# Another order for the first third of a planned kernel: small rows beside a weight's third

## The chip, the cores and the metric

The kernel runs on one core of a Trainium2 chip. The metric is the device time of one execution in microseconds (us), taken as the median of several runs. A core has five engines with a queue each, and each works its queue in order: PE multiplies matrices (PEld is its weight load), DVE, ACT and POOL do elementwise work, SP only issues transfers. ACT issues transfers too. The transfers themselves are carried by 16 DMA engines.

## What is computed

The first half is a linear attention with decay over 4 x 8 heads, 768 positions and 48 dimensions a head:

```
for t in range(S):
    cur = einsum('bhd,bhe->bhde', u * k[t], v[t])
    y[t] = einsum('bhd,bhde->bhe', r[t], state + cur)
    state = w[..., None] * state + einsum('bhd,bhe->bhde', k[t], v[t])
```

The second half takes y as x of shape (4, 768, 384), normalises each row with a gain g, and adds a two-layer network: `x + relu(norm(x) @ w1) @ w2`, with w1 of 384 x 1536 and w2 of 1536 x 384. Inputs and output are fp32; the kernel multiplies in bf16.

## The kernel before, in words

The positions are cut into 24 chunks of 128, six for each of the four batch entries. All work is written as small named steps. A string, PLAN, lists 895 of them as `name,index,engine`; the kernel emits them in exactly that order, and each engine and each transfer queue keeps it. The last letter gives the engine where there is a choice: v is DVE, s is ACT, g is POOL; for a transfer, s means that ACT issues it and a dash that SP does. So the order is a schedule, made ahead by a search and written out by hand.

The steps of one chunk i, in the order of their data:

- RA and RB load the two halves of r (96 KB each; packed rows, L410), KA and KB those of k for the chunks 0 to 3; LK loads all of k of a later chunk (L406), LV all of v (L437, 192 KB).
- SR and SK multiply r and k by powers of the decay (L217) into a bf16 tile `sc`; CV makes v bf16.
- TR transposes both on PE (L458, L462), TCr and TCk copy the result from PSUM to `trs` (L212). For the chunks 0 to 3, TB transposes k back (L476) and KC copies it into `sc` (L214), since the packed load has its rows in another order.
- Q multiplies the two transposed tiles, AT makes the scores on PE (L489), AM (in halves: AMa, AMb) masks them (L499).
- S on PE adds up the state and the weight of the present position (L520, L527, L533), CC copies the latter, ZU and ZD scale the state.
- VB is v times that weight (L552), Y the output of the attention on PE (L562, L570), X the sum of both (L577).
- SQ sums squares (L584), XN centres the row (L592), LT transposes it on PE (L626), XT copies it.
- UP is one part of the first layer (L641; PSUM tile `hp`), RL its relu (L657 on ACT, L659 on DVE), DN one third of the second layer (L669), OT the final sum (L725), STO the store.

Ahead of the chunks stand the constants. LE loads w (4 rows), LC 1 loads u (4 rows, L254) and LC 2 loads g (3 rows, L252), all tiny. LN takes the logarithm of w (L227), WBR spreads it over all partitions by a matmul (L240), PW, EK and ER make exponents of it, FKP and FR their exponentials (L357, L354). CR copies w into the tile `rows`, CT turns `rows` into columns with a matmul (L264), and CP copies those out. WBK is the other spreading matmul (L246), and FK and FN are its exponentials (L332, L337). WL makes the decay over a chunk (L368, L371). BD, UW and UGC make the rest.

The weights come in three parts of 768 KB each: LW1 n for w1 (L378), LW2 n for w2 (L395). SW scales w1 to bf16 in nine parts (three a third; L385 on ACT, L387 on DVE, L389 on POOL), CW copies w2 to bf16 in six. UP 0 needs the third 0 of w1, UP 2 the third 2, UP 1 the third 1; DN 0, 1 and 2 need the thirds of w2 of these numbers.

DU is a matmul of zeros, 512 columns wide (L316). It computes nothing; it keeps PE at work where nothing else is ready.

Transfers share eight semaphores in turn. A transfer therefore waits, on the engine that issues it, until the transfer eight places earlier in the plan has landed; what is queued behind it on that engine waits too.

The end of the function, which makes the order binding:

```
for step in PLAN.split():
    name, i, e = step.split(",")
    steps[name](int(i), e)
...
for ins in list(nc.cur_bb.bb.instructions)[traced:]:
    for chain in [ins.engine] + ["dma"] * ("dma" in type(ins).__name__.lower()):
        if chain in last:
            tc.add_manual_dep(ins, last[chain].name, in_order, reason="order of the plan")
        last[chain] = ins
```

Of the kernel before, what the change touches and what calls it, by code (L numbers as in the profile page):

```python
# [30 lines left out]
AT,3,- DN,0,- TB,3,- RL,18,s RL,1,s RA,5,- LK,5,- RA,8,s SQ,1,s ZU,2,v VB,2,v Q,3,v RB,5,- UP,17,- DN,1,- X,2,v SQ,2,s
UP,16,- RS,1,g SR,4,g CV,3,s RL,17,s KC,3,v AM,3,v LV,4,- RL,16,s DN,2,- RB,6,s RS,2,g SK,5,g RB,8,s XN,2,v Y,3,- LT,2,-
S,3,- CC,3,s LK,8,- SK,4,v OT,0,v XT,2,v RB,7,- LK,6,- VB,3,v DN,4,- TR,4,- RA,6,- UP,33,- TCr,4,s TCk,4,s ZU,3,v X,3,v
RL,33,s CV,4,s SQ,3,s UP,32,- DN,5,- LV,5,- RB,12,- RA,7,- XN,3,v Q,4,v SR,5,v AT,4,- LV,6,- S,4,- TR,5,- TCr,5,s DN,6,-
AM,4,v ZU,4,v OT,1,v SK,6,v SR,6,v TCk,5,s Y,4,- UP,34,- LT,3,- RB,11,- RB,13,s RL,32,s RA,12,s XT,3,s SR,8,g CC,4,s LK,7,s
VB,4,g AT,5,- DN,8,- RB,9,- Q,5,v TR,6,- DN,9,- S,5,- UP,49,- RL,34,s TCk,6,s AM,5,v SK,8,v UP,48,- LK,9,- TCr,6,s CV,5,s
RA,9,s RL,49,s RL,48,s TR,8,- AT,6,- CC,5,s TCk,8,s LV,7,- RA,13,- SR,7,v X,4,v RA,10,s RS,3,g CV,6,g VB,5,g Q,6,v XN,4,v
Y,5,- TCr,8,s AM,6,v UP,50,- DN,10,- S,6,- LT,4,- X,5,v SK,7,g XN,5,g RB,10,s XT,4,v SQ,4,s LK,10,s LK,14,s CC,6,s AT,8,-
Y,6,- RS,4,g SK,9,g ZU,6,v OT,2,v RL,50,v TR,7,- UP,66,- SQ,5,s VB,6,g RS,5,g CV,7,g DN,12,- TCk,7,s SR,9,g SR,10,g RL,66,s
TCr,7,s UP,65,- UP,64,- LT,5,- AM,8,v RA,16,- Q,8,v Q,7,v LK,11,s AT,7,- X,6,v XT,5,v RL,65,v DN,13,- LV,8,- LV,10,- RA,11,-  # L40
S,7,- DN,14,- CC,7,s AM,7,v OT,3,v ZU,7,v TR,9,- UP,81,- TCk,9,v SK,10,v Y,7,- VB,7,g STO,0,s XN,6,s RL,64,s TCr,9,s DN,16,-
RL,81,s ZD,7,v CV,8,g LV,9,- X,7,v S,8,- UP,80,- DN,17,- AT,9,- TR,10,- Y,8,- SK,11,v RA,14,- DN,18,- UP,82,- CC,8,v Q,9,v
XN,7,s LV,11,- ZU,8,v RL,80,s LK,12,s TCr,10,s CV,9,s TCk,10,s SQ,6,s VB,8,g SR,11,g AM,9,v LT2,6,- LV,13,s STO,1,- ZD,8,g STO,2,-
OT,4,v X,8,v LK,13,- LV,12,s SR,12,g S,9,- AT,10,- STO,3,- AM,10,v ZU,9,v TR,11,- SR,13,g DN,20,- Y,9,- RA,17,- XN,8,s TCr,11,s
RL,82,s CV,10,s CC,9,s TCk,11,v DN,21,- RB,16,s ZD,9,v Q,10,v Q,11,v VB,9,v LK,17,- UP,99,- AT,11,- RL,99,s S,10,- UP,96,- DN,22,-
UP,101,- CC,10,s X,9,v VB,10,g RL,96,s ZU,10,v OT,5,v SK,12,g CV,12,g RL,101,v S,11,- UP,97,- XN,9,s LT2,8,- CC,11,s TR,12,- Y,10,-
UP,100,- AM,11,v CV,11,g ZD,10,g SK,13,g CV,13,g RL,97,s UP,98,- TCr,12,s SQ,7,s TCk,12,v X,10,v RL,100,v XN,10,v Q,12,v RL,98,s DN,24,-
AT,12,- TR,13,- Y,11,- DN,25,- UP,113,- S,12,- RS,6,g LK,15,s RB,14,- LK,16,- LV,14,- RB,15,- RA,15,- VB,11,g LR,18,s RB,17,s RL,113,s
DN,26,- UP,115,- SQ,8,s TCk,13,v TCr,13,v X,11,v AM,12,v SK,14,g Q,13,g SR,14,g XN,11,s RL,115,s UP,114,- CC,12,v OT,6,v ZU,12,v LV,15,s
TKD,14,- SK,15,v SQ,11,s RL,114,s AT,13,- S,13,- DN,28,- TR,14,- UP,112,- DN,29,- TCr,14,s SR,15,g UP,116,- CC,13,v AM,13,v SK,16,v VB,13,g  # L50
RL,112,v ZU,13,v DN,30,- OT,7,v SQ,9,s SQ,10,s VB,12,g UP,117,- Y,13,- DN,32,- AT,14,- LT2,10,- LV,16,- TKD,15,- TKD,16,- ZD,13,g STO,4,s
Q,14,v LK,19,- LR,19,- X,13,v RL,117,v XN,13,v RS,7,g RL,116,s CV,14,s S,14,- DN,33,- TR,15,- Y,12,- SK,17,v TCr,15,s SR,16,g UP,131,-
X,12,v AM,14,v TKD,17,- DN,34,- UP,130,- STO,5,s RL,131,s LV,18,- RL,130,s XN,12,s LR,20,- Q,15,g TR,16,- AT,15,- Y,14,- CC,14,s CV,16,s
OT,8,v LT2,12,- SR,17,v RS,8,g TCr,16,v VB,14,v CV,15,g ZU,14,v LK,18,- UP,128,- DN,36,- UP,129,- DN,37,- Q,16,g S,15,- DN,38,- TR,17,-
AM,15,v X,14,v RL,128,v CC,15,s TCr,17,s SQ,13,s ZD,14,g SQ,12,s VB,15,g RL,129,v Q,17,g Y,15,- AT,16,- UP,132,- ZU,15,v OT,9,v UP,147,-
S,17,- DN,40,- X,15,v RL,132,s STO,6,s CC,17,v AM,16,v CV,18,s S,16,- UP,144,- XN,15,g ZD,15,g SK,18,g SR,18,g LV,17,- DN,41,- LV,19,-
STO,7,- STO,8,- XN,14,s RL,147,s UP,133,- AT,17,- LK,20,- RL,144,s Y,16,- UP,146,- RL,133,s DN,42,- UP,148,- ZU,16,v CV,17,v RL,146,v LT2,14,-
OT,10,v SR,19,v SR,20,v UP,145,- CC,16,s LK,22,s DN,44,- TKR,18,- ZD,16,g AM,17,v STO,9,- RS,9,g CV,19,g VB,16,g SQ,14,s LV,20,s RL,148,s
RL,145,s LR,22,- UP,149,- SK,19,g RL,149,s DN,45,- UP,165,- UP,163,- X,16,v LV,21,- RL,165,s TKR,19,- RL,163,s Y,17,- SK,20,v VB,17,g UP,160,-
DN,46,- Q,18,g X,17,v SQ,15,s XN,17,s OT,11,v UP,162,- RL,160,s S,18,- AT,18,- DN,48,- UP,161,- XN,16,v DN,49,- CC,18,v AM,18,v SR,22,g  # L60
# [720 lines left out]
```

## Time and profile before

| | us |
|---|---|
| median of three runs | 154.48 |
| lowest, highest run | 154.10, 155.49 |
| the profiled execution | 153.78 |
| its span, first to last instruction | 151.5 |
| busy PE, DVE, POOL, ACT | 143.4, 116.1, 92.2, 79.0 |
| mean granted clock of PE, as a share | 0.977 |

The profile is of one execution. The page gives busy times, a strip of 40 slices, the transfer queues, the chain of work that ended last and the costliest groups. Other views give the same trace as a timeline, as waits, as groups by shape, and as busy time in chosen stretches. A row of the timeline reads: start, duration, engine, line, operation, what is written and what is read, shapes, how many instructions, and in brackets how long the engine was idle before and what ended that. SPq and ACTq are the queues that issue transfers; the duration of such a row is that of the issue, not of the transfer.

### The profile page before, as it was taken

The numbers are of one execution on the slowest core, as the hardware profiler recorded it, in microseconds if no ns is written. First come the engines' busy times: TensorE is split into PE (matmuls) and PEld (weight loads), VectorE is DVE, ScalarE is ACT, GpSimd is POOL, SyncE is SP. The second block draws the span as 40 slices with busy tenths as digits, with TensorE's granted clock in tenths as the row PEclk, the third lists the DMA queues.
The fourth block names the chain that finished last, engine by engine and source line by source line (L and its number), as shares of the span: only waits on it lengthen the run. The fifth ranks groups of instructions, "written<-read, shape, count | busy, mean of one in ns | idle before, by whom it ended". The sixth has DMA issues, their size and how long they took to land.

```text
span 151.5 us, 4453 instructions
## 1 busy us (share of the span) xinstructions
PE 143.4 (95%) x1755; PEld 110.1 (73%) x1755; DVE 116.1 (77%) x239; ACT 79.0 (52%) x180; POOL 92.2 (61%) x136
## 2 busy tenths in 40 slices
PE   7399998999999999999999999999999999999991
PEld 2044576887888877888778788887777787878870
DVE  3365989998979998998989984967896738756511
ACT  2157776758886369564836194592438453220110
POOL 6204547962569948499986889954939982580000
PEclk9955999999999999999999999999999999999999
DMA  4988999888979859959998899999787631143012
GB/s 103 312 194 268 333 419 341 193 194 199 210 175 197 196 114 238 240 122 245 160 185 168 163 277 154 267 192 152 143 195 220 183 69 30 52 131 116 17 73 82
DMA packets 79389, 27.74 MB, mean 183 GB/s; under 512 B 68999, under 2 KB 77834, under 8 KB 79370
## 3 DMA queue, kind: packets, MB, share of 16 engines
...
q8 instruction: 13, 0.21, 0.6%
...
## 4 chain that ended last, share of the span: by engine, by line
PE 84%; DMA 8%; DVE 2%; POOL 2%; ACT 1%; issue 1%; ACTq 0%; POOLq 0%; DVEq 0%
PE hp L641 30%; PE o L669 30%; PE at L489 5%; DMA kf<-in_k_dram 5%; DMA rows<-in_moe_g_ln_dram 3%; PE y L570 3%; PE tr L458 3%; PE y L562 2%; PE s L533 2%; PE tr L462 2%; PE s L520 1%; PE s L246 1%; PE o L316 1%; POOL sc L217 1%; PE tr L626 1%
## 5 line engine op out<-in xcount | busy, mean ns | idle before, releaser
L641 PE MATMUL hp<-xT,w_sb 128*128 128x128 bf16 (+1 forms) x612 | 57.5, 241 | 0.2
L669 PE MATMUL o<-w_sb,hT 128*128 128x384 bf16 x276 | 55.7, 326 | 0.0
L641 PEld LDWEIGHTS <-w_sb 128*128 128x128 bf16 x612 | 49.0, 114 | 4.8 <-DVE w_sb L387 0.3
L657 ACT ACTIVATE hT<-hp 128x512 bf16<-128x512 f32 x51 | 30.1, 595 | 33.4 <-PE hp L641 30.4
L669 PEld LDWEIGHTS <-hT 128*128 128x128 bf16 x276 | 24.4, 97 | 10.3
L499 DVE TENSOR_TENSOR A<-at,mask 128x1024 bf16<-128x1024 f32 (+1 forms) x27 | 29.5, 1097 | 1.4 <-PE at L489 1.4
L552 POOL TENSOR_TENSOR Vb<-vf,cc 128x384 f32<-128x384 f32 x18 | 15.8, 880 | 9.1 <-DVE cc L214 3.3
L725 DVE SCALAR_TENSOR_TENSOR ot<-o,rs,x 128x384 f32<-128x384 f32 x23 | 14.1, 614 | 9.3 <-PE o L669 8.2
L212 ACT COPY trs<-tr 128x512 bf16<-128x512 bf16 x25 | 14.1, 588 | 11.9 <-PE tr L462 7.1
L217 POOL TENSOR_TENSOR sc<-rf,Fr 128x384 bf16<-128x384 f32 x11 | 11.3, 1033 | 12.2 <-DMA rf<-in_r_dram 8.1
L659 DVE TENSOR_SCALAR hT<-hp 128x512 bf16<-128x512 f32 x21 | 14.2, 686 | 5.2 <-PE hp L641 5.1
L584 ACT ACTIVATE sqj<-x,sm 128x384 bf16<-128x384 f32 x24 | 14.8, 617 | 5.4 <-DVE x L577 3.8
L577 DVE SCALAR_TENSOR_TENSOR x<-y,Vb 128x384 f32<-128x384 f32 x24 | 13.2, 552 | 4.3 <-PE y L570 2.0
L316 PE MATMUL o<-warm 128*128 128x512 bf16 x31 | 12.0, 499 | 1.1 <-DVE warm L271 1.1
L217 POOL TENSOR_TENSOR sc<-kf,Fk 128x384 bf16<-128x384 f32 x11 | 11.7, 1063 | 2.0 <-issue 2.0
L217 POOL TENSOR_TENSOR q<-trs 128x512 bf16<-128x512 bf16 x8 | 10.0, 1262 | 3.6 <-ACT trs L212 3.2
L601 POOL TENSOR_TENSOR rs<-rs,expo 128x1 f32<-128x1 f32 (+1 forms) x17 | 11.2, 657 | 1.4
L217 POOL TENSOR_TENSOR Z<-ZS,WLZ 128x384 bf16<-128x384 f32 x9 | 9.1, 1014 | 4.7 <-DVE ZS L546 4.7
L489 PE MATMUL at<-trs 48*128 48x128 bf16 x192 | 9.8, 222 | 0.0
L489 PEld LDWEIGHTS <-trs 48*128 48x128 bf16 x192 | 5.5, 96 | 4.9 <-issue 2.8
L570 PE MATMUL y<-vv,A 128*128 128x48 bf16 x192 | 8.7, 183 | 0.0
L217 DVE TENSOR_TENSOR q<-trs 128x512 bf16<-128x512 bf16 x16 | 7.3, 468 | 1.7 <-ACT trs L212 1.7
(101 smaller groups left out, 188.4 us busy)
## 6 DMA issues: line engine op xcount, KB each, us to landing
...
```

What stands on the lines that cost most here:

```text
L212: nc.scalar.copy(out=out, in_=in_)
L217: engines[e].tensor_tensor(out=out, in0=in0, in1=in1, op=ALU.mult)
L316: nc.tensor.matmul(out=warm_ps[0][:], lhsT=warm[:], rhs=warm[:].unsqueeze(1).to_broadcast([P, 4, P]), start=True, stop=True)
L489: nc.tensor.matmul(out=t[:, par, q, :], lhsT=trs(i)[p0 : p0 + D, 1, q, :], rhs=trs(i)[p0 : p0 + D, 0, q, :], start=True, stop=True,)
L499: nc.vector.tensor_tensor(out=AA(i)[:, a:b].rearrange("p e q t -> p (e q) t"), in0=psum["at", i][:, a:b].rearrange("p e q t -> p (e q) t") ...
L552: engines[e].tensor_tensor(out=Vb(i)[:].rearrange("p (h d) -> p h d", h=H), in0=vf(i)[:], in1=cc(i)[:].unsqueeze(2).to_broadcast([P, H, D] ...
L584: nc.scalar.activation(out=sqj[:], in_=xx(i)[:], func=ACT.Square, bias=sm[i][:], scale=-float(C), accum_out=sq[g][:, j : j + 1])
L641: nc.tensor.matmul(out=t[:, a * gw : (a + 1) * gw].rearrange("p (j t) -> p j t", j=size), lhsT=w1_sb[n][kc][:, fb::FB], rhs=xT(g)[:, :size ...
L657: nc.scalar.activation(out=o, in_=s, func=ACT.Relu)
L659: nc.vector.tensor_relu(out=o, in_=s)
L669: nc.tensor.matmul(out=psum["o", i][:, :C], lhsT=hT(g)[:, fk, j * P : (j + 1) * P], rhs=w2_sb[d][:, a, :], start=(fk == 0), stop=(fk == FK ...
L725: nc.vector.scalar_tensor_tensor(out=ot(i), in0=psum["o", i][:, :C], scalar=rs[g][:, j : j + 1], in1=xx(i)[:], op0=ALU.mult, op1=ALU.add,)
```

## The change

Only PLAN changes. The two plans hold the same 895 steps, each as often as before, with 31 DU in both. From its first row on the order differs. In the start-up:

- SP's first transfer is LE (ACT issued it), its second LW2 1 (it was its third). LC 2 is ACT's second transfer, and LC 1 its third.
- KA 0, RB 0 and KB 2 move to ACT's queue, RA 0 and RB 1 to SP's.
- RA 2 and RB 2 move behind LW1 0; RB 2 is issued by SP and RA 2 by ACT, behind KB 3 and WL.
- CR moves from DVE to POOL, CP from ACT to DVE; SR 0 moves to POOL, SR 2 to DVE, CW 2 to ACT, Q 0 to POOL, XN 0 to ACT, SK 1 to POOL.
- PE meets WBR after five DU (eight before), CT after two more (at once before), WBK after one more (two before); the last DU stands ahead of S 2 and LT 1 (behind both before).

In the whole plan XN has ACT for 15 chunks (9 before), RL has ACT 54 times (51), SK has POOL for 16 chunks (12), Q has POOL for 12 (8), SW has POOL for 3 parts (1).

The part of the diff that holds the start-up (the rest of the plan, down to the last store, is reordered likewise):

```diff
-LV,1,s LE,0,s MW,0,v MM,0,g MI,0,g DU,4,- DU,4,- KA,0,- RB,0,- LW2,1,- LC,1,s TL,0,s LC,2,s DU,4,- RA,0,s DU,4,- LN,0,s
-MP,0,v KB,0,- DU,4,- DU,4,- DU,4,- CR,0,v DU,4,- WBR,0,- CT,0,- DU,4,- RB,1,s CP,0,s KA,1,- LV,2,- PW,0,v ER,0,v EK,0,v
-FR,0,s FKP,0,s RA,2,s KB,1,- LV,0,- KB,2,- KA,2,- BD,0,g DU,4,- WBK,0,- SR,0,v SK,0,v CW,2,v RB,2,- CV,1,s WL,0,s RA,1,s
-SR,2,g UW,0,g TR,0,- DU,4,- DU,4,- LW1,0,- TCr,0,s TCk,0,s SK,1,v CW,3,v DU,4,- UGC,0,s RA,3,- KA,3,- Q,0,v CV,0,v DU,4,-
-LW1,2,- TB,0,- FK,0,s FN,0,s KC,0,s KB,3,s AT,0,- DU,4,- SR,1,v TR,1,- DU,4,- S,0,- DU,4,- TCr,1,s CC,0,s TCk,1,s AMa,0,v
-AMb,0,v SK,2,v RB,3,- CV,2,v DU,4,- Y,0,- DU,4,- VB,0,v X,0,v LW1,1,- AT,1,- TB,1,- DU,4,- DU,4,- SW,2,s SW,1,s SW,0,s
-SQ,0,s ZU,0,v KC,1,v LW2,0,- DU,4,- Q,1,g XN,0,g DU,4,- AMa,1,v SK,3,g S,1,- LT,0,- DU,4,- DU,4,- LW2,2,- CC,1,v XT,0,v
-DU,4,- VB,1,g AMb,1,v TR,2,- SW,6,v SW,8,v SW,7,v DU,4,- UP,0,- LV,3,- Y,1,- DU,4,- TCr,2,s TCk,2,s TB,2,- X,1,v XN,1,g
-RS,0,g ZU,1,v Q,2,v UP,2,- DU,4,- SW,3,g CW,0,g DU,4,- AT,2,- SR,3,v RL,0,s KC,2,s RL,2,s LT,1,- S,2,- DU,4,- SW,4,s
-SW,5,s XT,1,v CW,4,g CW,5,g TR,3,- UP,18,- LK,4,s AMb,2,v CC,2,v AMa,2,v TCk,3,s CW,1,s UP,1,- Y,2,- TCr,3,v RA,4,- RB,4,-
+MW,0,v LE,0,- LV,1,s DU,4,- LW2,1,- LC,2,s TL,0,s LC,1,s DU,4,- DU,4,- DU,4,- DU,4,- RB,0,s LN,0,s MM,0,g MI,0,g CR,0,g
+BD,0,g CV,1,g WBR,0,- DU,4,- DU,4,- MP,0,v PW,0,v CT,0,- RA,0,- KB,1,- EK,0,v CP,0,v ER,0,v KB,0,- KA,0,s UW,0,g DU,4,-
+WBK,0,- FKP,0,s RA,1,s FR,0,s DU,4,- SR,0,g DU,4,- LV,0,- RB,1,- LV,2,- KA,2,- KA,1,- CV,0,g CW,3,v SK,0,v FN,0,s KB,2,s
+UGC,0,s FK,0,s CW,2,s LW1,0,- KA,3,- RB,2,- LW1,2,- TR,0,- DU,4,- SK,1,g DU,4,- LW1,1,- TCr,0,s TCk,0,s KB,3,s DU,4,- DU,4,-
+TB,0,- WL,0,s RA,2,s CV,2,s SR,1,v KC,0,v Q,0,g RB,3,- RA,3,- DU,4,- DU,4,- TR,1,- AT,0,- SK,2,g S,0,- TCk,1,s AMb,0,v
+AMa,0,v DU,4,- DU,4,- DU,4,- CC,0,s TCr,1,s VB,0,g ZU,0,v LW2,0,- DU,4,- DU,4,- TB,1,- Y,0,- X,0,v LW2,2,- Q,1,v SR,2,v
+SW,2,v RA,5,- DU,4,- DU,4,- AT,1,- DU,4,- RB,4,- RA,4,- SW,0,s SW,1,s KC,1,s XN,0,s DU,4,- S,1,- LT,0,- DU,4,- SQ,0,s
+SK,3,g XT,0,s DU,4,- DU,4,- TR,2,- TCk,2,s TCr,2,s RA,6,- CC,1,v AMb,1,v DU,4,- UP,0,- LV,3,- ZU,1,v AMa,1,v DU,4,- Y,1,-
+AT,2,- SW,7,g SW,6,g TB,2,- RL,0,v VB,1,g SW,4,g SW,8,s X,1,v Q,2,v UP,2,- DU,4,- XN,1,g SW,3,s SW,5,s KC,2,v SR,3,g
+S,2,- LT,1,- UP,1,- LK,4,- SQ,1,s CC,2,s RL,2,s AMb,2,v XT,1,v TR,3,- AMa,2,v VB,2,g UP,18,- CW,0,v ZU,2,v RL,18,v CW,1,s
...
```

More of the change, by code (lines that the diff above doesn't have):

```diff
@@ L31 @@
[L31 to L60, printed above, removed]
@@ new lines @@
+CV,8,s TCr,7,s TCk,7,s LV,10,s CV,7,g SQ,5,s LK,11,- LK,13,- DN,13,- AT,7,- LT,5,- Q,7,v RL,66,s DN,14,- S,7,- XT,5,s AM,7,v
+RL,65,v TR,9,- UP,64,- SR,10,g CC,7,s CV,9,s TCr,9,s XN,6,s STO,1,s RL,64,s RA,13,s Y,7,- RA,11,- VB,7,g ZU,7,v SK,10,g TCk,9,v
+S,8,- UP,81,- X,7,v ZD,7,v XN,7,s CC,8,v RL,81,s LT2,6,- UP,82,- Y,8,- AT,9,- VB,8,g OT,3,v Q,9,v ZU,8,v RA,12,- UP,80,-
+DN,16,- TR,10,- SQ,7,s SQ,6,s RL,82,s TCr,10,s TCk,10,s STO,3,- RA,16,- S,9,- DN,17,- X,8,v CC,9,s AM,9,v LK,15,s SR,11,v CV,10,g
@@ new lines @@
+ZD,8,g VB,9,v LV,12,- LV,11,- Y,9,- DN,18,- RB,17,- SR,13,v SK,11,g UP,99,- TR,11,- RS,6,g RS,4,g AT,10,- RL,80,s XN,8,s X,9,v
+OT,4,v ZU,9,v Q,10,v LV,13,s SR,12,g RL,99,s UP,96,- UP,97,- DN,20,- TCk,11,s RL,96,s XN,9,s SK,12,g ZD,9,g LK,14,s S,10,- TCr,11,s
+AM,10,v CC,10,v DN,21,- Q,11,g ZU,10,v UP,101,- DN,22,- LT2,8,- STO,2,- VB,10,v RL,97,s SQ,8,s LV,14,s TR,12,- S,11,- AT,11,- CV,12,s
+RL,101,s RB,15,s RA,17,s RS,5,g OT,5,v TCr,12,s CV,11,g UP,98,- Y,10,- TCk,12,s ZD,10,g LV,15,- RL,98,s LK,16,s AM,11,v RA,15,- DN,24,-
@@ new lines @@
+AT,12,- X,10,v UP,100,- SK,13,g XN,10,s RL,100,s Q,12,v CC,11,v AM,12,v S,12,- TR,13,- DN,25,- UP,113,- Y,11,- CV,13,g VB,11,g LK,20,-
+LK,17,- CV,14,s RB,16,s TCr,13,s SQ,10,s DN,26,- ZU,12,v SR,14,v SK,14,v TCk,13,v TKD,14,- LV,16,- X,11,v Q,13,g UP,112,- XN,11,s LR,19,s
+CC,12,v AT,13,- OT,6,v STO,4,- S,13,- TR,14,- DN,28,- SR,15,v SK,16,v RL,113,s LR,18,s AM,13,v ZU,13,v CC,13,v RL,112,s UP,115,- SR,17,g
+SQ,9,s RL,115,s SQ,11,s UP,117,- DN,29,- Y,13,- ZD,13,v TCr,14,v VB,13,v DN,30,- RL,117,s UP,114,- TR,15,- AT,14,- UP,116,- OT,7,v X,13,v
```

44 lines of the change are left out of this document (31 added, 13 removed).

## The prediction

> **What bounds the kernel now.** I read the page's head first, then the busy time by stretch, then the waits, the chain and the timeline of the first 26 us.
>
> ```profile
> span 151.5 us, 4453 instructions
> PE 84%; DMA 8%; DVE 2%; POOL 2%; ACT 1%; issue 1%; ACTq 0%; POOLq 0%; DVEq 0%
> ```
>
> ```profile
> 5.10:7.80 2.70, 0.00 (x0) 0.00 (x1) 1.25 (x4) 0.00 (x0) 0.21 (x1) 1.00 0.99 340
> ...
> 10.70:14.80 4.10, 4.10 (x26) 2.20 (x25) 2.55 (x6) 2.69 (x6) 1.41 (x2) 0.50 0.93 274
> 14.80:25.35 10.55, 9.83 (x134) 6.63 (x133) 9.71 (x24) 7.67 (x15) 5.81 (x9) 1.00 1.00 367
> 25.35:147.80 122.45, 122.32 (x1582) 98.88 (x1581) 98.64 (x193) 64.82 (x150) 81.87 (x110) 1.00 0.78 166
> ```
>
> The columns of a stretch are length, busy PE, PEld, DVE, ACT, POOL, granted clock, DMA share, GB/s. From 25.35 us to 147.80 PE is busy 122.32 of 122.45 us: nothing is left to gain there, only to lose. So the time is the moment at which PE becomes full plus a fixed rest, and this change is worth what it does to that moment. In the first 25 us the DMA engines are the busy ones (0.93 to 1.00), and PE is fed with matmuls of zeros (L316, step DU). The change has the same 31 of them, and the same 895 steps, in another order.
>
> **Where the moment comes from.** PE turns full at TR 3 (25.35 us), behind LT 1 and S 2 (the first row, X 0 on DVE, is used further down):
>
> ```profile
> 17.39 0.56 DVE L577 SCALAR_TENSOR_TENSOR x<-y,Vb 128x384 f32<-128x384 f32 x1
> ...
> 24.35 0.34 PE L626 MATMUL tr<-ident,xn 128*128 128x128 bf16 x3 [0.42 <-POOL xn L592]
> ...
> 24.61 0.25 PE L520 MATMUL s<-uwI,q 128*128 128x2 bf16 x4
> ...
> 25.35 0.38 PE L458 MATMUL tr<-ident,sc 128*128 128x128 bf16 x4
> ```
>
> ```profile
> 2.80 4.89 DMA rows<-in_moe_g_ln_dram
> ...
> 13.94 6.89 DMA kf<-in_k_dram
> 21.00 1.02 POOL sc L217
> ```
>
> The chain names two late transfers: the g row (issued 2.80, landed 7.69), for which PE stands idle with CT, and KB 3 (issued 13.94, landed 20.83), which holds SK 3 and VB 1 on POOL, then X 1, XN 1 and LT 1.
>
> In the changed plan the last DU stands ahead of S 2 and LT 1, and nothing idle is planned behind them. LT 1 takes 0.26 us and S 2 with its matmuls runs to about 25.06. So the old time is met if the new S 2 starts 0.26 + 0.45 = 0.71 us ahead of 25.35, at 24.64 us. Each microsecond by which it starts later is one lost.
>
> **The rows and the first wait.**
>
> ```profile
> 1.96 0.78 ACTq L254 DMA_DIRECT2D rows<-in_u_dram  x1
> ...
> 2.06 0.59 SPq L395 DMA_DIRECT2D w_f<-in_moe_w_ch_dram  x1
> ...
> 7.83 0.43 PE L264 MATMUL s<-idr,rows 11*128 11x11 f32 x2 [2.75 <-DMA rows<-in_moe_g_ln_dram]
> ...
> 9.16 1.65 PE L246 MATMUL s<-ln_bd,ones 4*128 4x384 f32 x2
> ```
>
> The times to landing of four weight thirds, asked one by one: LW2 1 (issued 2.06), LW1 0 (10.68), LW2 0 (14.51), LW2 2 (17.22):
>
> ```profile
> DMA to landing us min/median/max: 5.3/5.3/5.3
> ...
> DMA to landing us min/median/max: 6.5/6.5/6.5
> ...
> DMA to landing us min/median/max: 10.0/10.0/10.0
> ...
> DMA to landing us min/median/max: 9.2/9.2/9.2
> ```
>
> LW2 1 lands at 7.36 and the g row at 7.69: the small row ends with the third beside it. After the change LE is SP's first transfer and LW2 1 its second, one issue (about 0.66 us) earlier, with two 96 KB transfers fewer ahead of it; at 340 GB/s those are 0.58 us, half of it within the start-up delay, so 0.3. It lands at 7.36 - 0.66 - 0.3 = 6.4, the u row 0.33 later, 6.7 (bounds: 6.1 when the 0.58 counts whole, 7.7 when the rows gain nothing). CT runs at 6.8 in place of 7.83; with one DU in place of two before WBK, WBK ends 2.5 us later, 9.3 (before: 10.81). CR moves to POOL and CP to DVE, each between waits for the rows; they cost nothing while the rows are last, and 0.2 us each if they are not. LE gates WBR; LN is free when the table load ends, about 3.0, so WBR and FKP come early and lie beside the wait for the rows. RA 1 on ACT waits for LW2 1 (same semaphore, two uses apart) with FR behind it, but FR needs ER, behind CP on DVE (about 8.0): no cost. TR 0 then stands near 10.0, 0.7 us earlier than before.
>
> **The new wait: RA 2.** A transfer waits until the one eight places earlier in the plan has landed. RB 1 on SP waits for the u row (LC 1), LV 0 for the g row (LC 2). From there the issues follow each other, about 0.6 us each:
>
> ```profile
> 8.31 0.54 ACTq L410 DMA_DIRECT2D rf<-in_r_dram  x1
> ...
> 10.68 0.64 SPq L378 DMA_DIRECT2D w_f<-in_moe_w_ch_dram  x1
> ...
> 13.80 0.67 SPq L378 DMA_DIRECT2D w_f<-in_moe_w_ch_dram  x1
> 13.94 0.54 ACTq L410 DMA_DIRECT2D kf<-in_k_dram  x1
> ```
>
> LV 0 (0.4 to 0.6, gone already if the g row lands early), RB 1, LV 2, KA 2, KA 1: LW1 0 at about 9.3, 1.4 us earlier than 10.68. KA 3, RB 2, LW1 2 follow; LW1 1 at 11.7, 2.1 us earlier. That is the gain. But KB 3 and RA 2 stand on ACT. Before, RA 2 was issued at 8.31, ahead of all of w1; now it stands behind WL, whose second instruction waits for its first, and so for the whole of ACT's queue:
>
> ```profile
> L212 ACT COPY trs<-tr 128x512 bf16<-128x512 bf16 x25 | 14.1, 588 | 11.9 <-PE tr L462 7.1 <-PE tr L458 4.1 <-DVE trs L214 0.6
> ...
> L212 ACT CAST w_sb<-w_f 128x768 bf16<-128x768 f32 x1 | 0.8, 837 | 0.0
> ...
> L337 ACT ACTIVATE Fn<-s,pow_n 128x384 f32<-128x384 f32 x1 | 0.6, 571 | 0.0
> L332 ACT ACTIVATE Fk<-s,pow_k 128x384 f32<-128x384 f32 x1 | 0.6, 562 | 0.0
> ```
>
> From WBK's end at 9.3: FN 0.57, FK 0.56, CW 2 (new on ACT) 0.84, TCr 0 and TCk 0 0.59 each, two short ones 0.4: 3.55, so RA 2 is issued at 12.9, 1.2 us behind LW1 1. Transfers of both queues landed nearly in the order of their issue: KB 3, issued 0.14 us after LW1 1 began, took 6.9 us although ACT's queue was otherwise empty. LW1 0 landed at 17.2 (10.68 + 6.5), KB 3 at 20.83; the 3.63 us hold LW1 2, four small ones and a part of LW1 1. A third alone takes 1.95 us (17.22 + 9.2 against 14.51 + 10.0). After: LW1 0 lands at 9.3 + 6.5 = 15.8, or with 5.3 as the shortest of the rows at 14.6; KB 3 3.6 later, 18.2 to 19.4; the rest of LW1 1 1.2 to 1.8; RA 2 0.3. That gives 19.7 to 21.5; I take 20.7, nearer to the row of LW1 0, which is the same transfer.
>
> SR 2 on DVE needs RA 2, and DVE is in order. Behind it stand SW 2, CC 1, AMb 1, ZU 1, AMa 1, RL 0, X 1, Q 2, KC 2, and then S 2 on PE waits for KC 2. TR 2, and UP 0 behind it, wait for SR 2 too.
>
> ```profile
> L659 DVE TENSOR_SCALAR hT<-hp 128x512 bf16<-128x512 f32 x21 | 14.2, 686 | 5.2 <-PE hp L641 5.1
> ...
> L577 DVE SCALAR_TENSOR_TENSOR x<-y,Vb 128x384 f32<-128x384 f32 x24 | 13.2, 552 | 4.3 <-PE y L570 2.0 <-POOL Vb L552 1.7
> L217 DVE TENSOR_TENSOR q<-trs 128x512 bf16<-128x512 bf16 x16 | 7.3, 468 | 1.7 <-ACT trs L212 1.7
> ...
> L217 DVE TENSOR_TENSOR sc<-rf,Fr 128x384 bf16<-128x384 f32 x7 | 4.7, 666 | 2.5 <-DMA vf<-in_v_dram 2.5
> L217 DVE TENSOR_TENSOR Z<-s,WLZ 128x384 bf16<-128x384 f32 x8 | 4.4, 549 | 0.0
> L499 DVE TENSOR_TENSOR A<-at,mask 128x512 bf16<-128x512 f32 x6 | 4.0, 677 | 0.0
> ...
> L387 DVE TENSOR_SCALAR w_sb<-w_f,g_neg 128x512 bf16<-128x512 f32 x3 | 2.0, 729 | 0.0
> ...
> L214 DVE COPY sc<-tr 128x512 bf16<-128x512 bf16 x2 | 0.8, 414 | 0.0
> ```
>
> 0.67 + 0.73 + 2 x 0.68 + 0.55 + 0.69 + 0.55 + 0.47 + 0.41 = 5.4, with two short ones and two hops between engines 0.2: S 2 starts 5.6 us after RA 2 lands, at 26.3. Against 24.64 that is 1.65 us lost. The 2 us gained for w1 are wasted: SW 0 and SW 1 are done long before SW 2. Had RA 2 been there when DVE asks (about 17.9: X 0 ended at 17.95 before, the front is about 0.6 earlier now, and Q 1 follows), S 2 would start at 23.5, a gain of 1.15 us.
>
> **The other moves.** By the rows' means the new engines take about 8 us from DVE (Q, SK, RL, SW, XN, XT), give ACT 8 (XN, XT, RL, CW) and POOL 4 (Q, SK). In 25.35:147.80 they are busy 98.6, 64.8 and 81.9 of 122.45 us, so the shifts lie beside PE and I cost them at nothing; if a slower POOL step (SK, Q) comes last somewhere, it costs a part of a microsecond each time: 0.5 at the upper end. LW2 0 and LW2 2 land near 24 and 26 as before (RB 3 on SP now waits for KB 2, but the DMA engines have LW1 1 to carry), ahead of DN 0. The transfers of chunks 3 to 8, on either queue, come behind them as before. The end of the plan differs by which engine does the last RL, with a matmul group as cover: nothing, 0.1 if not.
>
> **Sum.** Profiled execution 153.78 us (span 151.5) + 1.65 = 155.4. The median of the runs, 154.48, is 0.7 above the profiled execution; the forecast for a median is 154.48 + 1.65 = 156.1.
>
> **Rivals.**
> 1. Not slower: RA 2 passes the thirds. The place is ACT's queue; it decides at a landing of 19.0 us (24.64 - 5.6). Ahead of LW1 1, as KB 3 was in part, it lands at 18.5 to 19.4: 153.9 to 154.9. If it passes all of SP's backlog and lands by 17.9, the gain is the 1.15: 153.3. For it: the two queues are separate. Against: KB 3's 6.89 us.
> The Trainium skill, "DMA: Bandwidth & Descriptors", section "Queues, rings and completion order", says that each DMA engine goes round between the queues it has work for, packet by packet. By that rule RA 2 would go past SP's thirds and the time would be this rival's 153.3; KB 3's row disagrees.
> 2. The rows gain nothing (the u row is now issued wholly behind the third): CT stays at 7.8, RA 2 lands a microsecond later, 157.1.
> 3. The clock falls. PE idles about 1.5 us before TR 2 and again before Y 1. Before, 2.70 us without work at 5.1 to 7.8 was followed by a clock of 0.50. One spell at 0.50 of 3.4 us of PE work costs 1.7 more: 157.8. Against it: some matmuls stand between the two gaps.
> The Trainium skill, "TensorE: Matmul & The Clock Gate", section "What's actually happening", gives one idle window of about 3.4 us as what halves the clock; by it the two gaps would be too short and the rival falls away. Here 2.70 us idle sufficed, inside one such window that was not idle throughout.
>
> **How the numbers follow.** Forecast (RA 2 behind LW1 1) 0.52, its own range 155.2 to 157.0; rival 1 0.25, of which 0.1 at 153.3; rival 2 0.08; rival 3 0.15. A measurement here tells apart about 1%, 1.54 us: slower than 156.0 are a little over half of the forecast's cases (0.29) and rivals 2 and 3 (0.23): 0.52. Faster than 152.9 needs a gain beyond what any term gives: 0.06. Within 1%: 0.42. The range 153.8 to 158.0 leaves out the 153.3 case below (0.1) and, above, rival 3 together with a late RA 2 (under 0.1).
>
> **What would show it.** Right: an idle DVE up to SR 2, released by a transfer of r at 20 to 21 us; TR 2 near 21.5; S 2 near 26.3; w1's first third landed near 15; CT near 6.8. Wrong: SR 2 without a wait, with S 2 near 23.5; or PE idle after 27 us, where I have cost nothing.

## The result and the profile after

The changed kernel takes 153.27 us (median of 11 runs, 151.94 to 154.58), the kernel before, timed beside it, 154.62 us. The ratio is 0.990, 95% interval 0.987 to 0.993: faster by 1.0%. The forecast was 156.1 us, slower, with a range from 153.8; both the sign and the range were wrong. Here and below a median is of all executions, while a ratio leaves out the disturbed ones, those more than 1.5% above the fastest of their kernel.

The profiled execution of the changed kernel took 153.40 us with a span of 151.5 us, the same span as the profiled execution of before. First its head and its chain, then PE's two stretches around the moment at which it becomes full (columns as before: length, PE, PEld, DVE, ACT, POOL, granted clock, DMA share, GB/s):

```profile
span 151.5 us, 4441 instructions
PE 84%; DMA 8%; DVE 3%; ACT 2%; ACTq 1%; issue 0%; DVEq 0%
```

```profile
13.90:24.96 11.06, 9.32 (x135) 6.30 (x133) 7.92 (x18) 8.09 (x17) 6.99 (x9) 1.00 0.97 352
24.96:147.60 122.64, 122.59 (x1590) 99.48 (x1588) 98.20 (x189) 70.43 (x161) 82.40 (x105) 1.00 0.80 166
```

The picture is that of before: PE has gaps in the first 25 us (the last one over 0.1 us ends at 22.89) and none behind. The chain up to there has changed its links, though. KB 3 and POOL's SK 3 are gone from it. The u row and RA 2 have taken their place:

```profile
1.96 4.32 DMA rows<-in_u_dram
...
12.25 7.36 DMA rf<-in_r_dram
```

The timeline of the first 26 us, at the instructions that the prediction named:

```profile
6.42 0.57 PE L264 MATMUL s<-idr,rows 11*128 11x11 f32 x2 [0.87 <-DMA rows<-in_u_dram]
...
9.06 0.59 SPq L378 DMA_DIRECT2D w_f<-in_moe_w_ch_dram  x1
...
12.25 0.54 ACTq L410 DMA_DIRECT2D rf<-in_r_dram  x1
...
19.70 0.56 DVE L217 TENSOR_TENSOR sc<-rf,Fr 128x384 bf16<-128x384 f32 x1 [2.06 <-DMA rf<-in_r_dram]
...
20.32 0.40 PE L458 MATMUL tr<-ident,sc 128*128 128x128 bf16 x4 [1.14 <-DVE sc L217]
...
22.89 0.37 PE L570 MATMUL y<-vv,A 128*128 128x48 bf16 x8 [0.59 <-DVE A L499]
...
24.19 0.42 DVE L214 COPY sc<-tr 128x512 bf16<-128x512 bf16 x1
...
24.64 0.24 PE L520 MATMUL s<-uwI,q 128*128 128x2 bf16 x4
```

Read from the top: CT runs at 6.42, 1.4 us earlier than before. LW1 0 is issued at 9.06, 1.6 us earlier. RA 2 is issued at 12.25, behind WL on ACT, lands at 19.61, and DVE stands still for 2.06 us until SR 2 has it. TR 2 on PE waits for SR 2, and Y 1 (22.89) for AMa 1, which is behind SR 2 on DVE. From there PE has no gap, and S 2 starts at 24.64, just as KC 2 ends on DVE (24.19 + 0.42). So the new wait is there, as forecast; but S 2 starts exactly at the moment that the prediction worked out as parity (24.64), and the span is exactly that of before. PE's waits, in total us, times and longest, name the same step:

```profile
PE tr L458 <- DVE sc L217: 1.1, 1, 1.1
...
PE y L570 <- DVE A L499: 0.6, 1, 0.6
```

Two profiled executions of equal span, and yet medians 1.35 us apart: that is the second thing that the experiments had to explain.

### The profile page after: what moved, and what is told of

It reads as the page before. It is cut to its first block, busy times and chain, and to the rows that moved or that the text cites. A ratio compares the mean times of both kernels' runs of the same rounds, so it can differ in the third digit from the quotient of the medians.

```text
span 151.5 us, 4441 instructions
## 1 busy us (share of the span) xinstructions
PE 143.6 (95%) x1755; PEld 110.7 (73%) x1755; DVE 112.2 (74%) x225; ACT 85.4 (56%) x192; POOL 97.5 (64%) x138
## 4 chain that ended last, share of the span: by engine, by line
PE 84%; DMA 8%; DVE 3%; ACT 2%; ACTq 1%; issue 0%; DVEq 0%
PE hp L641 32%; PE o L669 30%; DMA rf<-in_r_dram 5%; PE at L489 5%; PE y L570 3%; DMA rows<-in_u_dram 3%; PE tr L458 2%; PE s L533 2%; PE y L562 2%; PE tr L462 2%; PE s L520 1%; PE s L246 1%; DVE A L499 1%; PE hp L684 1%; PE tr L626 1%; DVE w_sb L387 1%
## 5 line engine op out<-in xcount | busy, mean ns | idle before, releaser
L657 ACT ACTIVATE hT<-hp 128x512 bf16<-128x512 f32 x54 | 31.8, 597 | 29.7 <-PE hp L641 24.1
L552 POOL TENSOR_TENSOR Vb<-vf,cc 128x384 f32<-128x384 f32 x17 | 14.9, 874 | 8.8 <-ACT cc L212 6.8
L212 ACT COPY trs<-tr 128x512 bf16<-128x512 bf16 x27 | 15.1, 589 | 7.5 <-PE tr L462 5.6
L577 DVE SCALAR_TENSOR_TENSOR x<-y,Vb 128x384 f32<-128x384 f32 x24 | 13.3, 553 | 6.7 <-PE y L570 6.4
L584 ACT ACTIVATE sqj<-x,sm 128x384 bf16<-128x384 f32 x24 | 14.8, 616 | 2.6 <-DVE ot L725 2.2
L217 POOL TENSOR_TENSOR q<-trs 128x512 bf16<-128x512 bf16 x12 | 14.4, 1201 | 2.5 <-DVE trs L214 1.9
L659 DVE TENSOR_SCALAR hT<-hp 128x512 bf16<-128x512 f32 x18 | 12.3, 685 | 4.1 <-PE hp L641 4.0
L217 POOL TENSOR_TENSOR sc<-kf,Fk 128x384 bf16<-128x384 f32 x13 | 13.0, 1003 | 1.6 <-PE s L533 1.6
L217 POOL TENSOR_TENSOR Z<-ZS,WLZ 128x384 bf16<-128x384 f32 x8 | 8.2, 1026 | 5.9 <-DVE ZS L546 5.9
L217 POOL TENSOR_TENSOR sc<-rf,Fr 128x384 bf16<-128x384 f32 x10 | 10.7, 1068 | 1.6 <-PE tr L458 1.0
L590 ACT ACTIVATE xn<-x,sm 128x384 bf16<-128x384 f32 x15 | 9.3, 621 | 2.1 <-DVE x L577 1.9
L598 POOL TENSOR_SCALAR rs<-sq 128x1 f32<-128x1 f32 (+1 forms) x17 | 4.6, 269 | 8.0 <-ACT sqj L584 6.8
```

The source lines that it names most:

```text
L212: nc.scalar.copy(out=out, in_=in_)
L217: engines[e].tensor_tensor(out=out, in0=in0, in1=in1, op=ALU.mult)
L552: engines[e].tensor_tensor(out=Vb(i)[:].rearrange("p (h d) -> p h d", h=H), in0=vf(i)[:], in1=cc(i)[:].unsqueeze(2).to_broadcast([P, H, D] ...
L577: nc.vector.scalar_tensor_tensor(out=xx(i)[:], in0=psum["y", i][:, :C], scalar=1.0, in1=Vb(i)[:], op0=ALU.mult, op1=ALU.add, accum_out=sm[ ...
L584: nc.scalar.activation(out=sqj[:], in_=xx(i)[:], func=ACT.Square, bias=sm[i][:], scale=-float(C), accum_out=sq[g][:, j : j + 1])
L657: nc.scalar.activation(out=o, in_=s, func=ACT.Relu)
```

## The experiments

Medians (n is the number of runs of the kernel named), and ratios to the kernel before, timed beside it. Four groups were timed apart from each other: rows 1 to 4, 5 to 8, 9 to 12 and 13 to 15. Between groups compare the ratios.

| kernel | median us (n) | ratio, 95% interval | S 2 starts at | RA 2 issued, landed |
|---|---|---|---|---|
| before_again | 154.56 (10) | 0.9987, 0.9940 to 1.0033 | 22.51 | 7.41, 10.79 |
| after_again | 153.10 (10) | 0.9917, 0.9877 to 0.9957 | 23.93 | 12.46, 19.05 |
| start_after | 154.10 (12) | 0.9942, 0.9894 to 0.9989 | 24.44 | 12.34, 19.85 |
| start_before | 157.26 (6) | 1.0183, 1.0113 to 1.0254 | 24.30 | |
| ra2_early | 151.99 (6) | 0.9833, 0.9781 to 0.9884 | 22.84 | 10.77, 15.32 |
| kb3_early | 154.16 (12) | 0.9977, 0.9936 to 1.0017 | 24.05 | |
| front_after | 153.92 (12) | 0.9943, 0.9903 to 0.9983 | 23.76 | 12.14, 18.73 |
| front_before | 153.86 (12) | 0.9950, 0.9904 to 0.9997 | 24.76 | |
| ra2_late | 154.42 (10) | 1.0001, 0.9960 to 1.0042 | 24.50 | 14.39, 19.98 |
| third_behind | 152.73 (6) | 0.9891, 0.9853 to 0.9929 | 23.97 | 12.85, 17.36 |
| engines_back | 164.43 (6) | 1.0595, 1.0538 to 1.0651 | 23.96 | 12.18, 18.97 |
| engines_fwd | 166.59 (6) | 1.0753, 1.0703 to 1.0802 | 24.40 | 8.07, 10.89 |
| rest_mended | 153.54 (12) | 0.9952, 0.9906 to 0.9999 | 22.94 | 8.38, 11.48 |
| front_mended | 153.71 (12) | 0.9934, 0.9889 to 0.9979 | 24.37 | 12.07, 18.96 |
| ra2_sto0 | 151.79 (6) | 0.9838, 0.9787 to 0.9889 | 22.16 | 10.71, 14.75 |

The times of S 2 and RA 2 are those of the one profiled execution of each.

### The two kernels again

Both kernels, unchanged, for a second profile.

> The plan before once more, for a second profile of it. Its first profiled execution (153.78 us, span 151.5) lies 0.84 us under its median of 154.62. Theory (the moment at which PE becomes full, set by KB 3's landing, varies from run to run): a profile whose time is nearer the median shows TR 3 later than 25.35 us by about as much as the span is longer than 151.5, and KB 3 landing later than 20.83. Rival (the part behind 25 us varies): TR 3 at 25.3 again, and the difference behind it.

> The changed plan once more, for a second profile. Theory: RA 2 lands at 19.0 to 20.2 us, S 2 starts 5.0 us later, at 24.0 to 25.2, and the span follows S 2 by 126.9 us (151.5 - 24.64). Rival (the front varies with the clock's window, not with the transfer): S 2 moves by a half microsecond or more while RA 2's landing stays at 19.6.

The medians repeat. In the second profile of the changed kernel RA 2 landed at 19.05 and S 2 started 4.9 us behind it, at 23.93, but the span of 151.3 follows S 2 by 127.4 us and not by 126.9.

The second profile of before is the important one, and it is neither what the theory nor what the rival said: this execution (152.67 us) lies further below the median than the first. S 2 starts at 22.51 us, 2.1 earlier than in the first, without any edit, and KB 3 landed at 17.75 in place of 20.83. KB 3 is not where the 2.1 us come from: PE is ahead by 0.89 us at CT (6.94, as both rows had landed at 6.70), by 2.1 at TR 0 (8.60 in place of 10.73), and only then is KB 3 issued (11.82 in place of 13.94). Between CT and TR 0 stand two DU, whose rows last 0.63 us in the first profile and 0.38 in the second, and WBK. But the span is only 0.8 shorter (150.7). Since both executions run the same matmuls in the same order, the nth matmul of one can be set against the nth of the other. The lead is 2.0 us at 24 to 31 us, 1.56 at 33, 1.17 behind 52, and 0.75 from 139 on. So before does stand still behind 25 us in this execution; the profile read for the prediction had next to none of it. Two of the places, DVE and then PE:

```profile
45.03 0.56 DVE L217 TENSOR_TENSOR Z<-s,WLZ 128x384 bf16<-128x384 f32 x1 [0.59 <-ACT cc L212]
45.50 0.61 DVE L725 SCALAR_TENSOR_TENSOR ot<-o,rs,x 128x384 f32<-128x384 f32 x1
...
137.71 0.62 DVE L725 SCALAR_TENSOR_TENSOR ot<-o,rs,x 128x384 f32<-128x384 f32 x1 [0.79 <-DMA out_dram<-ot]
```

```profile
46.16 0.81 PE L669 MATMUL o<-w_sb,hT 128*128 128x384 bf16 x4 [0.37 <-DVE ot L725]
...
138.38 0.81 PE L669 MATMUL o<-w_sb,hT 128*128 128x384 bf16 x4 [0.27 <-DVE ot L725]
```

At 45 us OT 2 stands on DVE behind ZU 6, which waits for ACT, and PE's DN waits for OT 2. At 138 us OT 21 waits until STO 17 has landed (issued 133.45, landed 137.59), since both use the same buffer. The store of 192 KB took 1.9 us in two profiles with this rest, 3.5 in one and 4.1 in two (before_again and kb3_early). OT 21 has slack for the first, just enough for the second (in the first profile it starts 0.12 us after the landing), and PE stands still for 0.27 and 0.29 us with the last. Neither wait was seen in the changed kernel's two profiles; its second has another, 0.41 us at 48.94, where AT 7 waits for ACT.

### Is it RA 2? ra2_early and ra2_late

ra2_early moves one step of the changed plan, RA 2, from ACT behind WL to SP behind RB 2:

```diff
-RB,2,- LW1,2,-
+RB,2,- RA,2,- LW1,2,-
...
-WL,0,s RA,2,s CV,2,s
+WL,0,s CV,2,s
```

> The changed plan with one step moved: RA 2 is issued by SP right behind RB 2, ahead of LW1 2 and LW1 1 (it was on ACT behind KB 3 and WL). Theory (RA 2's place behind the two thirds sets S 2): RA 2 lands at 15.5 to 17.8, SR 2 runs at 17.7 to 18.3 without a long wait, S 2 starts at 23.4 to 24.2 (next late: VB 1 on POOL, behind SW 7 and SW 6, which wait for LW1 2), 0.3 to 0.9 us faster than the changed plan. Rival (another chain sets S 2): S 2 stays within 0.2 us of 24.3 and so does the time.

```profile
17.60 0.55 DVE L217 TENSOR_TENSOR sc<-rf,Fr 128x384 bf16<-128x384 f32 x1
...
22.84 0.24 PE L520 MATMUL s<-uwI,q 128*128 128x2 bf16 x4
```

SR 2 has no wait any more, S 2 starts 1.8 us earlier than in the changed kernel's first profile (1.1 than in its second), and the ratio falls from 0.990 and 0.992 to 0.983, which is 1.0 to 1.3 us: more than the 0.3 to 0.9 expected. So RA 2's place does cost the changed kernel time, and one moved step beats both kernels. It costs less than the prediction had it: S 2 at 26.3 in place of 23.5, or 2.8 us. PE now has no wait over 0.1 us between CT (6.52) and S 2.

ra2_late goes the other way: RA 2 on SP behind RA 3, so behind all of w1.

```diff
-WL,0,s RA,2,s CV,2,s
+WL,0,s CV,2,s
...
-RB,3,- RA,3,-
+RB,3,- RA,3,- RA,2,-
```

> The changed kernel with RA 2 issued by SP behind RA 3, that is behind all three thirds of w1 and two more small loads. If the first third ends where RA 2's landing puts it: landing about 22.3 in place of 19.1 to 19.6, SR 2 released by it, S 2 5.0 us later at 27.2, median 1 us per us, 2.6 to 3.2 later than the changed kernel: 155.8 to 156.4. Rival (PE has cover between, so that only a part comes through): 153.5 to 155.

```profile
20.00 0.56 DVE L217 TENSOR_TENSOR sc<-rf,Fr 128x384 bf16<-128x384 f32 x1 [1.93 <-DMA rf<-in_r_dram]
...
24.50 0.24 PE L520 MATMUL s<-uwI,q 128*128 128x2 bf16 x4
```

RA 2 was issued 2.1 us later and landed 0.4 later, at 19.98 and not 22.3; the last third of w1 had landed at 19.13 in this execution. S 2 at 24.50 is where the changed kernel has it (24.64 and 23.93). The ratio is 0.8 to 1.0% over the changed kernel's, and the median of 154.42 is in the rival's range, but not by the rival's cover: the landing itself hardly moved. Nor does the profile show where the time goes: its PE ends at 148.10, 0.26 later than the changed kernel's. So this run says nothing on what a later landing would cost. That a transfer issued into this backlog lands when the backlog has drained, whenever it is issued, is an inference; the edit also changed RA 2's queue.

### Is it KB 3? kb3_early

The kernel before with KB 3, the late transfer of its chain, on SP behind KA 3:

```diff
-FK,0,s FN,0,s KC,0,s KB,3,s AT,0,-
+FK,0,s FN,0,s KC,0,s AT,0,-
...
-RA,3,- KA,3,- Q,0,v
+RA,3,- KA,3,- KB,3,- Q,0,v
```

> The plan before with one step moved: KB 3 is issued by SP right behind KA 3, ahead of LW1 2 and LW1 1 (it was on ACT behind KC 0). Theory (the plan before was limited by the same kind of place): KB 3 lands near 17.8 in place of 20.8, SK 3 follows at once, TR 3 starts up to 1 us earlier, 0.3 to 1.0 us faster than before. Rival: within 0.3 us of before, as the rest waits for w2 or for DVE anyway.

KB 3 landed at 18.09, S 2 started at 24.05, between the two profiles of before. The wait for KB 3 is gone, but something else holds S 2 at once: PE is busy without a gap from CT, which still waits for the g row (7.84), up to S 2. The ratio's interval, 0.9936 to 1.0017, holds 1, and it holds the 0.994 of the changed front (further down) too, so this run neither shows nor excludes that KB 3's wait is a part of what the change takes away.

### What is the third beside the rows worth? third_behind

ra2_early with LW2 1 moved from the second place of SP to behind KB 1, so that the small rows go alone:

```diff
-LV,1,s DU,4,- LW2,1,- LC,2,s
+LV,1,s DU,4,- LC,2,s
...
-RA,0,- KB,1,- EK,0,v
+RA,0,- KB,1,- LW2,1,- EK,0,v
```

> The changed kernel with RA 2 early as in ra2_early, and w2's third moved from SP's second place to behind KB 1, so that the small rows no longer end with it. Theory one (the rows are on the chain, 4.4 us of it): u and g rows land by 5.2, CT by 5.4 in place of 6.5, S 2 about 0.5 to 1 earlier than 22.8, median 151.0 to 151.6. Theory two (the bytes of the first 22 us bound w1 and so SW 2 and UP 0, and zeros' matmuls fill PE whatever the rows do): CT early, w1 landed where it was to 0.3 us, S 2 at 22.6 to 23.0, median 151.8 to 152.2.

The rows of third_behind, then the same two issues of ra2_early:

```profile
8.48 0.54 SPq L410 DMA_DIRECT2D rf<-in_r_dram  x1
...
10.99 0.59 SPq L378 DMA_DIRECT2D w_f<-in_moe_w_ch_dram  x1
```

```profile
6.40 0.53 SPq L410 DMA_DIRECT2D rf<-in_r_dram  x1
...
8.90 0.59 SPq L378 DMA_DIRECT2D w_f<-in_moe_w_ch_dram  x1
```

Both theories were wrong. The rows did land early (g 3.40, u 4.75, against 5.80 and 6.39), and CT ran at 5.47, 1.05 earlier. But LW2 1 landed at 8.28 in place of 5.88, and RB 0, now issued 0.3 us behind it, at 8.47 in place of 6.77. RB 0 stands eight places ahead of RB 1, which waits for it on SP (in ra2_early it waits for the u row, landed 6.39). Everything behind RB 1 is issued 2.1 us later, w1 lands 1.7 to 2.0 later, and S 2 starts at 23.97, 1.1 later. The ratio is 0.6% above ra2_early's. So here the third beside the rows costs them about 1 us and buys 2 us for w1.

### Front or rest? Four mixed plans

Each takes one plan up to a step and the steps that are left in the other plan's order: start_after has the changed order up to LT 1, front_after up to TR 4 (the first 211 steps); start_before has the order before up to the last DU, front_before up to TR 4 (the first 214).

> The changed plan up to LT 1, then the remaining steps in the order and on the engines of the plan before. Theory (the start makes the difference): 1.0 to 1.5 us faster than before, as the changed plan is. Rival (the order and the engines behind 25 us make it): within 0.4 us of before.

> The plan before up to its last DU, then the remaining steps as in the changed plan. Theory (the start makes the difference): within 0.4 us of before. Rival (the rest makes it): 1.0 to 1.5 us faster than before.

> The changed plan up to TR 4 (about 33 us), then the remaining steps as in the plan before. Theory (the gain is made in the start): 1.0 to 1.5 us faster than before. Rival (it is made behind it, by the other order and engines): within 0.4 us of before.

> The plan before up to TR 4 (about 33 us), then the remaining steps as in the changed plan. Theory (the gain is made in the start): within 0.4 us of before. Rival (behind it): 1.0 to 1.5 us faster than before.

start_before came out 2.8 us slower, outside theory and rival, and says nothing on the question. At its seam the steps do not fit, and PE waits for w1's scaling, which neither kernel has:

```profile
PE hp L641 <- POOL w_sb L389: 2.1, 2, 1.2
```

The other three lie between theory and rival, and agree: the changed front alone gives 0.9942 and 0.9943, the changed rest alone 0.9950, and 0.9943 times 0.9950 is 0.9893, about the whole (0.990 and 0.992). The intervals are as wide as the halves, 0.4 to 0.5% to either side, so "about half" is the best estimate and not more. But a part of the gain lies in the rest, to which the prediction had given nothing.

### What is it in the rest?

The plans differ there in order and in engines. engines_back keeps the changed order and gives each step of DVE, ACT and POOL from TR 4 on the engine it has before (101 steps differ); engines_fwd is the converse (99 steps). An excerpt of the first:

```diff
-UP,34,- TCr,4,s RB,12,s XN,3,s RL,32,s TCk,4,v
+UP,34,- TCr,4,s RB,12,s XN,3,v RL,32,s TCk,4,s
```

> The changed kernel with its own order throughout, but from TR 4 on each of 101 steps of DVE, ACT and POOL (14 RL to DVE and 9 away from it, Q, SR, XN, VB, CC, CV) on the engine that it has in the kernel before; loads keep their queues. Theory (in the rest it is the lighter DVE that pays: PE waited 0.4 to 0.7 us for DVE's ot in profiles with the old rest): DVE busy about 116 us instead of 112, the wait PE o <- DVE ot comes back, median 153.7 to 154.1 beside 153.2 for the changed kernel, ratio to the kernel before about 0.995. Rival (the order of the rest pays, the engines do not): 153.0 to 153.4, ratio 0.990 to 0.992. Second rival (an engine choice only fits its own order): over 154.5, with new waits of PE named in the profile.

> The kernel before with its own order throughout, but from TR 4 on each of 99 steps of DVE, ACT and POOL on the engine that it has in the changed kernel. Theory (the lighter DVE pays): no wait PE o <- DVE ot, median 153.9 to 154.2, ratio 0.995 to 0.997. Rival (the order pays): 154.4 to 154.8, ratio 0.999 to 1.001. Second rival (the choice only fits its own order): over 155, with new waits of PE.

Only the second rival was near: each choice of engines fits its own order and no other. Both came out 10 to 12 us slower, with waits of PE all over the rest; the three largest of engines_back:

```profile
PE s L520 <- DVE q L217: 2.9, 4, 1.7
PE hp L641 <- ACT hT L657: 1.7, 3, 0.8
PE hp L641 <- DVE hT L659: 1.4, 1, 1.4
```

So these two runs do not tell whether a lighter DVE makes the rest better: order and engines cannot be taken apart this way. That leaves single waits. rest_mended is the kernel before with the two of them that its profiles show taken away, and front_mended is front_after with the same edit:

```diff
-ZU,6,v OT,2,v
+OT,2,v ZU,6,v
...
-OT,17,v ZU,22,v
+OT,17,v STO,17,- ZU,22,v
...
-STO,18,- STO,17,-
+STO,18,-
```

> The kernel before with two steps moved, both behind 25 us: OT 2 on DVE ahead of ZU 6 in place of behind it (ZU 6 waits 0.6 to 0.8 us for ACT's cc, and PE then 0.4 to 0.6 for OT 2 at 46 to 48 us), and STO 17 on SP right behind OT 17 (it was landed 0.12 us ahead of OT 21 in three of five profiles with this rest, and PE then stood still at 138 us). Theory (PE does wait behind 25 us in the usual execution of before, and single waits of this kind are the rest's half of the gain): both waits of PE gone, median 0.6 to 0.9 below before, ratio 0.994 to 0.996. Rival (the waits only move on to the next step, so that the rest's half lies elsewhere): ratio 0.998 to 1.001.

> The changed order up to TR 4, then the order before with the same two steps moved (OT 2, STO 17). Theory: both halves together without the new rest, median 153.1 to 153.4, ratio 0.990 to 0.992, as the changed kernel. Rival (the new rest does something else): 153.8 to 154.1 as front_after, ratio 0.994 to 0.996.

rest_mended came out at 0.9952, inside the theory's 0.994 to 0.996, but the interval ends at 0.9999, and its profile (of an execution of 154.99 us, above the median) does not bear the theory out. The wait at 138 us (0.27 and 0.29 us where it was seen) is gone. The one at 46 us has only moved on by one step, to the relu behind OT 2, as the rival had it:

```profile
PE hp L641 <- DVE hT L659: 0.6, 1, 0.6
```

front_mended, at 0.9934, lies between theory and rival, and its interval holds both; beside front_after's 0.9943 the two moved steps are worth 0.1% there, and the wait at the relu is in its profile too (0.5 us).

All profiles together say the same. From 26 to 147 us PE stands still for 0.1 to 1.0 us in the five with the rest of before (mean 0.65: before, before_again, start_after, kb3_early, front_after), and for 0.05 to 0.7 us in the six with the new rest (mean 0.50: after, after_again, front_before, ra2_early, ra2_late, third_behind). Their difference of 0.15 us is a fifth of the 0.8 us that the rest is worth by front_before. So single waits of PE are seen, but that they are the rest's half is not shown.

### A wait of the new rest: ra2_sto0

Set against the changed kernel matmul by matmul, ra2_early leads by 1.81 us at 23 to 46 us, by 1.39 at 47.6 and by 0.9 from 49 on. Half of what its front gains is given back at two places. ACT in ra2_early there, and PE:

```profile
42.96 2.58 ACTq L732 DMA_DIRECT2D out_dram<-ot  x1
45.58 0.60 ACT L657 ACTIVATE hT<-hp 128x512 bf16<-128x512 f32 x1 [2.15 <-issue]
```

```profile
46.23 0.83 PE L641 MATMUL hp<-xT,w_sb 128*128 128x128 bf16 x12 [0.26 <-ACT hT L657]
...
48.12 0.40 PE L489 MATMUL at<-trs 48*128 48x128 bf16 x8 [0.41 <-ACT trs L212]
```

The issue of the first store, STO 0, holds ACT for 2.58 us, where most issues take 0.4 to 0.6. It did so in all eight profiles in which STO 0 stands at this place of the new rest (1.23 to 2.59 us), at a time when the DMA engines are busy nearly throughout. The relu RL 50, XN 5, CV 8 and the copies TCr 7 and TCk 7 are queued behind it. ra2_sto0 moves STO 0 behind TCk 7 on ACT:

```diff
-ZU,6,v STO,0,s TR,7,-
+ZU,6,v TR,7,-
...
-TCr,7,s TCk,7,s LV,10,s
+TCr,7,s TCk,7,s STO,0,s LV,10,s
```

> The changed kernel with RA 2 early as in ra2_early, and STO 0, the first store, moved on ACT behind TCk 7: its issue held ACT for 1.2 to 2.6 us at 43 to 46 us in five profiles with the new rest, while the DMA engines were full, and RL 50, TCr 7 and PE behind it. Theory (the front's gain is given back there: 0.9 of 1.8 us between ra2_early and the changed kernel): the waits of PE at 46 and 48 us (0.67) gone, PE's end at 146.0 to 146.4, median 151.2 to 151.6, ratio 0.978 to 0.981. Rival (the full DMA engines give the loads back late whatever ACT issues, so that another wait takes the place): 151.8 to 152.2.

```profile
span 148.9 us, 4442 instructions
```

```profile
44.49 0.38 ACTq L732 DMA_DIRECT2D out_dram<-ot  x1
```

The issue takes 0.38 us, both waits of PE are gone, and the lead over the changed kernel at 23 us (2.49 here) is still 2.50 at the end. Of the 1.6 us by which PE ends earlier than in ra2_early (145.34 against 146.95), 0.9 is this and 0.7 is an earlier front of this one execution. In that front PE has no wait over 0.1 us behind CT in either profile, and the two orders are the same; what differs is when the DU go over from rows of 0.63 us to rows of 0.38: at 12.0 us here, behind 13.4 in ra2_early. The profile shows what the moved step does; the times do not: the median of 151.79 is short of the theory's 151.2 to 151.6, and the ratios are 0.9838 and 0.9833, the other way round. Either version beats both kernels, by 1.6 to 1.7% against before. Why the issue was held is open. The DMA engines were as busy around the short issue as around the long one (busy share 1.2 in both, a little over 1 as the profile counts it); it also came 3.5 us behind ACT's transfer before it, and the long one 1.3.

## Why the prediction was wrong

**The front up to RA 2's issue: right.** CT was forecast at 6.8 and ran at 6.42, TR 0 at 10.0 and ran at 9.86, LW1 0 landing at 15.8 and landed at 15.27, RA 2's issue at 12.9 and was at 12.25. The mechanism was right too: RA 2 behind WL, DVE idle until it lands, TR 2 and S 2 late. Its price was put too high: 2.8 us forecast against RA 2 being there, 1.1 to 1.8 us measured at S 2 (ra2_early).

**The term of the sum: mis-sized, 1.65 us forecast, 0.0 measured.** "I take 20.7", and then "S 2 starts 5.6 us after RA 2 lands, at 26.3". RA 2 landed at 19.61 (18.73 to 19.85 in the five other profiles that have it at this place), 1.1 us earlier: issued 0.65 earlier, and landed not behind LW1 1 but 2.1 us ahead of it (21.69). From the landing to S 2 it took 5.0 us and not 5.6, since means of whole rows were added up end to end, while consecutive DVE instructions in the timeline start before the one ahead has ended by its row (the 0.56 us of Z at 45.03 is followed by OT at 45.50). Together 1.66 us: S 2 at 24.64, the parity worked out beforehand, and the spans came out equal. So the parity rule held in this pair of executions and its input was wrong. In the five other profiles S 2 starts at 23.76 to 24.44, so the term is rather below nothing than above.

**"Nothing is left to gain there, only to lose", and the moves behind 25 us "at nothing": wrong.** This was read from one execution of before, in which PE was busy 122.32 of 122.45 us behind 25.35. That execution belongs to the fastest quarter: its span is 151.5 us, while the 80 executions of before that the ratios use have a median span of 152.1 (half of them within 151.6 to 152.6). For the changed kernel 19 have a median of 151.2 (half within 150.6 to 151.4), and its profiled one, 151.5 too, lies above the upper quarter. So equal spans of two profiles hid 0.9 us. The sentence that treats the 0.7 us between the median and the profiled execution as a constant failed with it: beside this result the median of before is 0.84 us above its profiled execution, that of the changed kernel 0.13 below its own. The other profiles of before's rest show single waits of 0.3 to 0.6 us that come and go with the landing of a store or of ACT's cc, so PE does stand still behind 25 us; the new rest gave 0.995. What in the new rest gives it is not shown.

**The rivals.** Rival 1 ended nearest, at 153.3 to 154.9. That the median meets its 153.3 is luck: that case needed RA 2 past all of SP's backlog and landed by 17.9. RA 2 passed the last third clearly (landed 21.69) and the one ahead of it by 0.17 us only (LW1 2, issued 10.92, landed 19.78); it landed 7.36 us after its issue. The Trainium skill, "DMA: Bandwidth & Descriptors", section "Queues, rings and completion order", has each DMA engine go round between its queues packet by packet. By that, if the turns of both queues moved as much, a 96 KB transfer alone on ACT's queue but for KB 2 and KB 3 should not have had to wait out most of SP's backlog. The 7.36 us, beside 2.96 for the same transfer ahead of w1 (issued 8.31, landed 11.27, in before), disagree with that, and in these 7.36 us ACT's queue moved 0.28 MB and SP's 2.28; the passing of the last third agrees with the rule. How much a turn moves, no run here shows. Rival 2 was wrong: CT ran at 6.2 to 6.6 us in all profiles with the changed plan's start but third_behind (5.47), and at 6.9 to 7.9 in those with the start of before. Rival 3 was wrong: the granted clock is 1.00 in each stretch from 13.9 us to 147.60.

**What stays open.** Which step saves the front's half of the gain (0.9943 for front_after) is not shown. The profiles of the two mixed plans with the new front do not help: their spans, 152.1 and 152.2 us, lie above the medians of their kernels (151.3 and 151.5). S 2 does not show it either: 22.5 to 24.8 us in six profiles with the old start, 23.8 to 24.6 in six with the new one. It need not be KB 3 (kb3_early).

The speed of PE in the first 16 us is a rival that no run tests. The profile's clock column does not settle it, nor does the mean clock of an execution. The column says 1.00 up to the first change that the trace records, yet a DU's row lasts 0.63 us there, as at the 0.50 that the first profile of before shows from 7.98 to 14.80 us, and 0.38 us later. The trace records the rise to 1.00 that ends this at 14.8 and 12.2 us in the two profiles of before and at 13.9 to 16.1 in the five others with its start; with the changed start at 12.0 to 14.8 us in ten profiles, with a median of 13.6 in place of 15.4. Nor is it settled which waits, if any, are the rest's half.
